# A fused decode block, forward and backward: hf, relu, mask and masked gradient made in three groups of column blocks

## The chip, the core and the metric

The kernel runs on one core of a Trainium2 chip. The metric is device microseconds (us) of one execution, as the median of several runs. The core has five engines that run their own instruction streams in order and wait for one another by semaphores: TensorE (PE, matmuls, with its weight loads shown apart as PEld), VectorE (DVE), ScalarE (ACT), GpSimd (POOL) and SyncE (SP, which here only issues transfers). Transfers run on 16 DMA engines that all queues share.

## The reference, cut to what matters

A pre-norm attention block over a key and value cache, a relu MLP, and the gradient of all inputs for a given output gradient. The batch B is 2, one query position, H = 32 heads of size 128, 4096 cached positions, model width D = 640 and MLP width Dff = 1728.

```python
h  = x + attention(layernorm(x), k_cache, v_cache, wq, wo)
h2 = h + relu(layernorm(h) @ w1) @ w2          # out_0
grads = vjp(x, k_cache, v_cache, wq, wo, w1, w2)(grad_out)   # out_1 .. out_7
```

Nearly all bytes are the cache (K and V, 1 MB for each of the 64 pairs of batch row and head) and its two gradients of the same size. The value cache is needed twice: for the output, and again for the gradient of the scores. The kernel keeps a few V tiles and loads 52 of them a second time.

## The kernel before, in words

**Two passes and a middle.** Pass 1 (`p1_iter`) has rows i = 0 to 65, one for each pair of batch row and head. A row transposes the K tile of pair i on PE, makes its scores, forms the products `pk` of the exponentials and K for pair i-1 on DVE (line 470, two halves), and multiplies V of pair i-2 on PE. Pass 2 (`p2_iter`, index j) reads V again (tile W), makes the score gradients and the two cache gradients gV and gK on DVE (line 844), and stores both through POOL's DMA queue. Between them, for each batch row b, lies the middle (`middle_gen(b)`): attention output, the layernorm, `hf` (the MLP's hidden row before the relu), relu, mask, the masked gradient `ghfc`, the gradient through w1, the layernorm's backward, and then for each group of heads the gradient through wo (`go_group`), without which pass 2 can't begin for those heads.

**Where a row stands.** The middle of batch row 0 runs beside rows 34 to 65 of pass 1; pass 2 begins at row `P2_AT` = 41 whatever the middle has done (what is missing for its first head is forced at that point) and then takes one step every second row. From there rows of pass 1 and steps of pass 2 alternate on all engines. After row 65 pass 2 runs alone, 14 of its 64 steps done; beside it run the middle of batch row 1, and then, once its sums over w1 are done (mark `("w1", 1)`), the generators `fin_gen` (outer products for the weight gradients, stores on ACT's queue) and `gx_gen` (gradient through wq).

**The order is written out by a small planner.** All engines get their instructions in the order in which the Python generators are stepped. A row of pass 1 has eight steps. After each, `bg_step` gives the middle a credit (0.8 a step from row 34 on, `RATES`); each `yield` of the middle costs what it says (0.25 for a column block of hf, 0.85 or 0.9 for a sum, 0.5 for a bare `yield`). `wait(n)` holds the middle for n steps (2n once `spread` is 2, from row 41 on). Sums over w1 and wo (`ttr`, line 678: multiply and add along a row) also need a slot (`turn()`): five a row in rows 34 to 40, two slots (with a pass-2 step) or one from row 41 on.

**The part around the change.** `hf` has 14 column blocks (13 full and one of 64). Each is five matmuls with one column (line 778). The relu (lines 781 and 783), mask (786) and masked gradient (787) follow on DVE over all 14. Then `wait(3)`. Then three times: `spread_some` turns five (the last time four) columns of `ghfc` into a row on all partitions, with PE transposes (line 645) and one ACT copy (line 647) into one half of `fbc`; and five sums over w1 (line 800). The layernorm's backward (`ln_bwd`) and `go_group` follow. In `go_group` each head is one sum over wo (line 699); then come a cast and a product (701, 703), two matmuls and four copies (`pair_rows`, 340 and 345), further matmuls (708, 712) and five small DVE operations (714 to 720).

**PSUM banks.** `pst` hands out banks by role. `hf_ps` and other small results use bank 7 (`mid`). The rows of `spread_some` use role `bc`: banks 2 and 7 by turns in rows 34 to 40, bank 7 alone for batch row 1.

**Buffers.** Loads of K, V and W take one of 13 large buffers (`ld`) and are issued by SP in one list as buffers come free (`pump`); K's buffer comes free after the second half of `pk`. Around row 41 some buffers go over to gV and gK (`g`), and later to `f` and `q`.

Of the kernel before, what the change touches and what calls it, by code (L numbers as in the profile page):

```python
# [9 lines left out]
ALU = mybir.AluOpType  # L10
# [5 lines left out]
def kernel(  # L16
# [20 lines left out]
    nc = tc.nc  # L37
# [6 lines left out]
    ND = D // 128  # L44
    NSC = Sk // 128
    NFF = Dff // 128
    F_rem = Dff - NFF * 128
    NF = NFF + (1 if F_rem else 0)
# [9 lines left out]
    def f_kc(c):  # L58
        return 128 if c < NFF else F_rem
# [11 lines left out]
    banks = {"tps": [0, 1], "sps": [2, 3, 4], "m": [5], "u": [6], "mid": [7], "bc": [7]}  # L71

    def pst(shape, dtype, role, name):

        k = banks[role].pop(0)
        banks[role].append(k)
        return ps.tile(shape, dtype, tag=f"bank{k}", bufs=1, name=name)
# [63 lines left out]
    def wait(n):  # L141

        end = step[0] + n * spread[0]
        while step[0] < end and not forced[0]:
            yield 0.0
        yield
# [34 lines left out]
    x2c = cols.tile([128, ND, B], BF16)  # L181
# [4 lines left out]
    acol = cols.tile([128, NF, B], BF16)  # L186
    ghfc = cols.tile([128, NF, B], BF16)
# [15 lines left out]
    ga = cols.tile([128, B, NF], FP32)  # L203
# [128 lines left out]
    w1_t = wts.tile([128, ND, Dff], BF16)  # L332
# [265 lines left out]
    def o_group():  # L598
        b, g = divmod(o_next[0], H // OG)
        hs = slice(g * OG, g * OG + OG)  # L600
        nc.vector.tensor_tensor(out=OU[:, b, hs], in0=OU[:, b, hs], in1=rt[:, b, hs], op=ALU.mult)
        nc.vector.tensor_copy(out=OFc[:, hs, b], in_=OU[:, b, hs])
        o_next[0] += 1

    def a_group():

        b, g = divmod(a_next[0], H // OG)
        a_ps = pst([128, ND], FP32, "mid", "a_ps")
        for c in range(ND):
            for h in range(g * OG, g * OG + OG):  # L610
                nc.tensor.matmul(a_ps[:, c:c + 1], lhsT=wo_t[:, h, c * 128:(c + 1) * 128], rhs=OFc[:, h, b:b + 1],
                                 start=(h == g * OG), stop=(h == g * OG + OG - 1))
        nc.vector.tensor_tensor(out=asum[:, b, :], in0=asum[:, b, :], in1=a_ps[:], op=ALU.add)
        a_next[0] += 1
# [10 lines left out]
    def u_out(b):  # L625

        t = pst([128, H], FP32, "mid", "uc_ps")
        nc.tensor.matmul(t[:], lhsT=u4[0], rhs=fold[:], start=True, stop=True)
        nc.vector.tensor_tensor(out=Uc[:, b, :], in0=t[:], in1=rt[:, b, :], op=ALU.mult)


    def wide_row(name):
        return cols.tile([128, B * D], BF16, tag="wide_row", name=name)

    def later_heads():

        return P_bf[:, B * H - D // NSC:, :].rearrange("p h s -> p (h s)")

    def spread_some(colsrc, c0, n, kc_of, dst):

        t = pst([128, D], BF16, "bc", "bcb_ps")
        w = 0
        for c in range(c0, c0 + n):
            kc = kc_of(c)
            nc.tensor.transpose(t[:, w:w + kc], colsrc[0:kc, c:c + 1].to_broadcast([kc, 128]), ident_bf[0:kc, 0:kc])
            w += kc
        nc.scalar.copy(out=dst[:, 0:w], in_=t[:, 0:w])
        return w
# [28 lines left out]
    def ttr(in0, in1, acc, width, junk, kc=128):  # L677
        nc.vector.tensor_tensor_reduce(out=junk[0:kc, 0:width], in0=in0, in1=in1, scale=1.0, scalar=0.0,  # L678
                                       op0=ALU.mult, op1=ALU.add, accum_out=acc)
# [3 lines left out]
    def turn():  # L683

        while slot[0] <= 0:
            yield 0.0
        slot[0] -= 1

    def one(src, b):
        return src[:, :, b]  # L690
# [61 lines left out]
    def middle_gen(b):  # L752
        if o_next[0] < (b + 1) * H // OG:
            o_group()
        u4[0] = wide_row("u")[:, 0:256].bitcast(FP32)
        nc.vector.tensor_reduce(out=u4[0], in_=u_bank[0][:].rearrange("p (s d) -> p d s", s=4),
                                axis=AX.X, op=ALU.add)
        yield
        while a_next[0] < (b + 1) * H // OG:
            if a_next[0] == o_next[0]:  # L760
                o_group()
                yield
                yield
            a_group()
            yield
        at_bf = small.tile([128, ND], BF16, tag="at_bf", bufs=1, name="at_bf")
        nc.vector.tensor_copy(out=at_bf[:], in_=asum[:, b, :])
        nc.vector.tensor_tensor(out=h1c[:, :, b], in0=xg32[:, b, :], in1=at_bf[:], op=ALU.add)
        h32 = small.tile([128, 1, ND], FP32, tag="h32", bufs=1, name="h32")
        nc.vector.tensor_copy(out=h32[:, 0, :], in_=h1c[:, :, b])  # L770
        yield ("a", b)
        u_out(b)
        yield from ln_fwd(h32[:], 1, x2c[:, :, b:b + 1], rstd2[:, b:b + 1])
        hf_ps = pst([128, NF], FP32, "mid", "hf_ps")
        for cf in range(NF):
            kc = f_kc(cf)
            for c in range(ND):
                nc.tensor.matmul(hf_ps[0:kc, cf:cf + 1], lhsT=w1_t[:, c, cf * 128:cf * 128 + kc],
                                 rhs=x2c[:, c, b:b + 1], start=(c == 0), stop=(c == ND - 1))
            yield 0.25  # L780
        nc.vector.tensor_scalar(out=acol[:, 0:NFF, b], in0=hf_ps[:, 0:NFF], scalar1=0.0, scalar2=None, op0=ALU.max)
        if F_rem:
            nc.vector.tensor_scalar(out=acol[0:F_rem, NFF, b:b + 1], in0=hf_ps[0:F_rem, NFF:NF],
                                    scalar1=0.0, scalar2=None, op0=ALU.max)
        mask = small.tile([128, NF], FP32, tag="mask", bufs=1, name="mask")
        nc.vector.tensor_single_scalar(out=mask[:], in_=acol[:, :, b], scalar=0.0, op=ALU.is_gt)
        nc.vector.tensor_tensor(out=ghfc[:, :, b], in0=ga[:, b, :], in1=mask[:], op=ALU.mult)
        yield from wait(3)
        fbc = wide_row("fbc")
        gx2 = small.tile([128, 1, ND], FP32, tag="gx2", bufs=1, name="gx2")  # L790
        gx2p = small.tile([128, ND, 3], FP32, tag="gx2p", bufs=1, name="gx2p")
        first_f = 0
        for k, n in enumerate((ND, ND, NF - 2 * ND)):
            row = fbc[:, (k % 2) * D:(k % 2 + 1) * D]
            w = spread_some(one(ghfc, b), k * ND, n, f_kc, row)
            yield
            for c in range(ND):
                yield from turn()
                part = w1_t[:, c, first_f:first_f + w]
                ttr(part, row[:, 0:w], gx2p[:, c, k:k + 1], w, part if b else later_heads())  # L800
                yield 0.85
            first_f += w
        nc.vector.reduce_sum(out=gx2[:, 0, :], in_=gx2p[:], axis=AX.X)
        yield ("w1", b)
        yield from ln_bwd(gx2[:], x2c[:, :, b:b + 1], rstd2[:, b:b + 1], gc[:, :, b:b + 1], gh1c[:, :, b:b + 1], 1)
        row = wide_row("hbc")
        hbc, junk = row[:, 0:D], row[:, D:2 * D]
        spread_some(one(gh1c, b), 0, ND, lambda c: 128, hbc)
        yield
        yield ("gh1", b)  # L810

        first = H - KEPT[b]
        bounds = [(first, first + 2), (first + 2, H)] if b == 0 else [(first, H)]
        bounds += [(h, min(first, h + GH)) for h in range(0, first, GH)]
        for h0, h1 in bounds:
            yield from go_group(b, h0, h1, hbc, junk)
        if b > 0:
            yield from mlp_out()
# [401 lines left out]
    for n, (i, j) in enumerate(plan):  # L1220
# [42 lines left out]
        if i is None:  # L1263
            spread[0] = 2
            at_k[0] = 1
            k = 0
# [28 lines left out]
        if i is not None and i in (H + 1, NP1 + 1):  # L1295
            bg.append((f"m{i // H - 1}", middle_gen(i // H - 1)))
# [41 lines left out]
```

## Time and profile before

| | |
|---|---|
| median of 3 runs | 889.0 us (888.36 to 891.58) |
| profiled execution, its own time | 888.48 us |
| span of the profiled execution | 886.3 us |
| busy share of the span: PE, DVE, ACT, POOL | 83%, 77%, 56%, 23% |
| bytes moved, mean rate | 361.85 MB, 408 GB/s |
| rows 34 to 41 of pass 1 begin at | 210.2, 217.4, 225.9, 232.0, 237.9, 243.6, 249.6, 256.0 us |

The row starts are read from the chain of waits, at each row's matmul of line 515. The span is what the trace shows from the first to the last instruction; the profiled execution's own time is 2.2 us longer. Tables by stretch give, for each stretch of the span, the busy time of each engine, the TensorE clock that was granted, the DMA engines' busy share and the rate. In lists in order of time the first two columns are start and duration in us. The brackets at the end say how long the engine was idle before the instruction, and what ended that.

### The profile page before, as it was taken

The numbers are of one execution on the slowest core, as the hardware profiler recorded it, in microseconds if no ns is written. First come the engines' busy times: TensorE is split into PE (matmuls) and PEld (weight loads), VectorE is DVE, ScalarE is ACT, GpSimd is POOL, SyncE is SP. The second block draws the span as 40 slices with busy tenths as digits, with TensorE's granted clock in tenths as the row PEclk, the third lists the DMA queues.
The fourth block names the chain that finished last, engine by engine and source line by source line (L and its number), as shares of the span: only waits on it lengthen the run. The fifth ranks groups of instructions, "written<-read, shape, count | busy, mean of one in ns | idle before, by whom it ended". The sixth has DMA issues, their size and how long they took to land.

```text
span 886.3 us, 24732 instructions
## 1 busy us (share of the span) xinstructions
PE 738.8 (83%) x10143; PEld 618.2 (70%) x10143; DVE 681.3 (77%) x1281; ACT 498.8 (56%) x1292; POOL 204.1 (23%) x358
## 2 busy tenths in 40 slices
PE   4999899999999997988868767787877899867690
PEld 4887788888887886877757656665656667564550
DVE  2666787877788896876778887878788689989861
ACT  1444343446776664654536767777656766545570
POOL 1344433343312010000011332222222111111220
PEclk9999999999999999998995655555566755555555
DMA  9999999999879999999999999999999999999996
GB/s 380 423 420 414 417 409 417 425 423 412 332 295 402 423 423 426 422 426 425 414 398 396 418 421 421 420 413 420 419 416 403 417 425 420 425 425 425 425 424 275
DMA packets 56289, 361.85 MB, mean 408 GB/s; under 512 B 5680, under 2 KB 11760, under 8 KB 15472
## 3 DMA queue, kind: packets, MB, share of 16 engines
q1 hardware_dynamic: 34520, 211.13, 57.8%
q0 software_dynamic: 18432, 134.23, 36.5%
q10 hardware_dynamic: 3224, 14.92, 4.1%
q8 instruction: 80, 1.31, 0.5%
q14 instruction: 33, 0.27, 0.1%
HBM read 211.11 MB, written 149.13 MB: 406 GB/s over the span
## 4 chain that ended last, share of the span: by engine, by line
PE 35%; DMA 34%; DVE 16%; ACT 7%; issue 5%; SPq 0%; POOL 0%; ACTq 0%; POOLq 0%; DVEq 0%
DMA Vt<-in_A_v_cache_dram 15%; PE t_ps L424 14%; DMA out_dram<-gK 11%; PE m_ps L460 9%; DVE gK L844 4%; DVE gV L844 4%; DMA out_dram<-gV 3%; ACT gV L930 3%; PE s_ps L437 3%; DMA wqs<-in_A_wq_dram 3%; DVE pk L470 2%; PE u_ps L498 2%; ACT t_sb L429 2%; PE dp_ps L437 2%; DVE gxj L678 2%
## 5 line engine op out<-in xcount | busy, mean ns | idle before, releaser
L429 ACT COPY t_sb<-t_ps 128x512 f32<-128x512 f32 x479 | 273.1, 587 | 192.4 <-PE t_ps L424 188.6
L437 PEld LDWEIGHTS <-t_sb 128*128 128x128 bf16 x4096 | 178.9, 102 | 63.8 <-ACT t_sb L429 36.2
L424 PE MATMUL t_ps<-ident_f,Wt 128*128 128x128 f32 x832 | 198.6, 389 | 0.9 <-ACT t_sb L429 0.9
L470 DVE TENSOR_TENSOR pk<-Kt,ep 128x2048 bf16<-128x2048 bf16 (+1 forms) x128 | 152.6, 1193 | 47.1 <-ACT ep L524 29.0
L460 PE MATMUL m_ps<-pk,Vt 128*128 128x129 bf16 x2048 | 172.0, 223 | 19.9 <-DMA Vt<-in_A_v_cache_dram 18.8
L844 DVE TENSOR_TENSOR gK<-rb,gsp 128x2048 bf16<-128x2048 bf16 x128 | 153.4, 1227 | 13.3 <-DMA out_dram<-gV 8.5
L460 PEld LDWEIGHTS <-Vt 128*128 128x128 bf16 x2048 | 125.6, 99 | 50.2 <-issue 28.4
L424 PEld LDWEIGHTS t_ps<-ident_f,Wt 128*128 128x128 f32 x832 | 138.2, 202 | 31.9 <-issue 25.2
L424 PE MATMUL t_ps<-ident_f,Kt 128*128 128x128 f32 x1024 | 156.0, 286 | 2.5 <-DMA Kt<-in_A_k_cache_dram 1.9
L844 DVE TENSOR_TENSOR gV<-rb,pp 128x2048 bf16<-128x2048 bf16 (+1 forms) x128 | 142.7, 1139 | 16.3 <-DMA out_dram<-gK 9.9
L486 POOL COPY pk<-ep 128x16 bf16<-128x16 bf16 x80 | 83.6, 1046 | 158.4 <-ACT ep L524 80.0
L424 PEld LDWEIGHTS t_ps<-ident_f,Kt 128*128 128x128 f32 x1024 | 113.9, 145 | 5.0 <-ACT t_sb L429 2.7
L437 PE MATMUL dp_ps<-gom,t_sb 128*128 128x2 bf16 x2048 | 96.0, 168 | 25.1 <-ACT t_sb L429 24.7
L931 POOL DMA_DIRECT2D out_dram<-gV x62 | 33.0, 533 | 305.3 <-DVE gsp L858 135.1
L437 PE MATMUL s_ps<-qm,t_sb 128*128 128x2 bf16 x2048 | 87.4, 164 | 1.5 <-DVE t_sb L427 1.5
L986 ACT CAST ot<-o_ps 128x512 bf16<-128x512 f32 (+3 forms) x152 | 67.5, 491 | 8.4 <-DMA out_dram<-ot 5.2
L588 ACT CAST MT<-m_ps 128x128 bf16<-128x128 f32 x64 | 17.0, 266 | 94.5 <-PE m_ps L460 94.4
L899 POOL DMA_DIRECT2D out_dram<-gK x53 | 28.2, 533 | 135.4 <-DVE gK L844 104.9
L882 ACT ACTIVATE rb<-dp_ps,rt 128x256 bf16<-128x256 f32 x64 | 30.2, 472 | 44.7 <-PE dp_ps L877 43.4
L678 DVE CUSTOM_DVE_ANT_0 hbc<-wo_t,hbc 128x640 bf16<-128x640 bf16 x64 | 52.8, 825 | 0.3
L678 DVE CUSTOM_DVE_ANT_0 gxj<-wqs,gqr 128x1024 bf16<-128x1024 bf16 x40 | 48.7, 1217 | 1.0 <-DMA wqs<-in_A_wq_dram 0.8
L930 ACT ACTIVATE gV<-rb,pa 128x128 bf16<-128x128 bf16 x152 | 46.5, 392 | 3.9 <-DMA out_dram<-gK 3.9
(205 smaller groups left out, 758.2 us busy)
## 6 DMA issues: line engine op xcount, KB each, us to landing
Kt<-in_A_k_cache_dram SPq DMA_DIRECT2D x64, 1024.0 KB, 19.4
Vt<-in_A_v_cache_dram SPq DMA_DIRECT2D x64, 1024.0 KB, 15.5
out_dram<-gV POOLq DMA_DIRECT2D x64, 1024.0 KB, 14.9
out_dram<-gK POOLq DMA_DIRECT2D x64, 1024.0 KB, 15.0
Wt<-in_A_v_cache_dram SPq DMA_DIRECT2D x52, 1024.0 KB, 11.6
wq_t<-in_A_wq_dram SPq DMA_DIRECT2D x5, 1024.0 KB, 7.8
wo_t<-in_A_wo_dram SPq DMA_DIRECT2D x4, 1280.0 KB, 17.6
wqs<-in_A_wq_dram SPq DMA_DIRECT2D x5, 1024.0 KB, 22.3
```

The source lines that it names most:

```text
L424: nc.tensor.transpose(t_ps[:, j, :], natf[:, 2 * cc:2 * cc + 2, :].rearrange("p c k -> p (c k)"), ident_f[:])
L429: nc.scalar.copy(out=t_sb[:], in_=t_ps[:])
L437: nc.tensor.matmul(dst[:, sc:sc + 2], lhsT=v[:, j, :, par], rhs=vecs[:, par, :], start=(par == 0), stop=(par == 1))
L460: nc.tensor.matmul(r["m"][:, 0:129], lhsT=r["V"][:, sc, :], rhs=r["pk"][sc // HALF][:, sc % HALF, 0:129], start=(sc == 0), stop=(sc == NSC ...
L470: nc.vector.tensor_tensor(out=p["pk"][k][:, 0:n, 0:128].rearrange("p s (a two) -> p s a two", two=2), in0=p["K"][:, sl, :].rearrange("p s ...
L486: nc.gpsimd.tensor_copy(out=col, in_=e)
L678: nc.vector.tensor_tensor_reduce(out=junk[0:kc, 0:width], in0=in0, in1=in1, scale=1.0, scalar=0.0, op0=ALU.mult, op1=ALU.add, accum_out=acc)
L844: nc.vector.tensor_tensor(out=pairs_view(dst[:, sl, :]), in0=row.rearrange("p (a two) -> p a two", two=2)[:, None, :, :].to_broadcast([128 ...
L882: nc.scalar.activation(out=rb[:], in_=bank[:, 128:384], func=ACT.Copy, scale=rt[:, b, h:h + 1])
L930: nc.scalar.activation(out=gV[:, NSC - act + k, :], in_=c["rb"][:, 0:128], func=ACT.Copy, scale=pa[:, k:k + 1])
L931: nc.gpsimd.dma_start(out=natural(out_3, b, h), in_=gV[:])
L986: nc.scalar.copy(out=ot[0:P, k, n0:n0 + nn], in_=o_ps[0:P, 0:nn])
```

## The change

The 14 column blocks are cut in three groups (5, 5 and 4), the same that the sums use. The generator now gives: hf of group 0, its relu, mask and masked gradient; hf of group 1, the spread of group 0, relu, mask and masked gradient of group 1; hf of group 2 and its relu part; then the sums of group 0, and spread and sums of groups 1 and 2. `wait(3)` is gone, and the bare `yield` between the first spread and its sums. The roles of the PSUM banks are set so that the spread of group 0 doesn't use the bank of `hf_ps`: for batch row 0 the list is turned until bank 7 is not first, for batch row 1 `bc` is bank 5 until the sums are done. `P2_AT` stays 41. The number of matmuls, copies, sums and transfers stays the same; DVE has 12 more small operations (six for each batch row).

```diff
-        for cf in range(NF):
-            kc = f_kc(cf)
-            for c in range(ND):
-                nc.tensor.matmul(hf_ps[0:kc, cf:cf + 1], lhsT=w1_t[:, c, cf * 128:cf * 128 + kc],
-                                 rhs=x2c[:, c, b:b + 1], start=(c == 0), stop=(c == ND - 1))
-            yield 0.25
-        nc.vector.tensor_scalar(out=acol[:, 0:NFF, b], in0=hf_ps[:, 0:NFF], scalar1=0.0, scalar2=None, op0=ALU.max)
...
-        yield from wait(3)
...
-        for k, n in enumerate((ND, ND, NF - 2 * ND)):
+        parts = [(0, ND), (ND, 2 * ND), (2 * ND, NF)]
+
+        def hf_part(k):
+            for cf in range(*parts[k]):
+                kc = f_kc(cf)
+                for c in range(ND):
+                    nc.tensor.matmul(hf_ps[0:kc, cf:cf + 1], lhsT=w1_t[:, c, cf * 128:cf * 128 + kc],
+                                     rhs=x2c[:, c, b:b + 1], start=(c == 0), stop=(c == ND - 1))
+                yield 0.25
+
+        def relu_part(k):
+            c0, c1 = parts[k]
+            full = min(c1, NFF)
+            nc.vector.tensor_scalar(out=acol[:, c0:full, b], in0=hf_ps[:, c0:full], scalar1=0.0, scalar2=None, op0=ALU.max)
...
+            nc.vector.tensor_single_scalar(out=mask[:, c0:c1], in_=acol[:, c0:c1, b], scalar=0.0, op=ALU.is_gt)
+            nc.vector.tensor_tensor(out=ghfc[:, c0:c1, b], in0=ga[:, b, c0:c1], in1=mask[:, c0:c1], op=ALU.mult)
+
+        def spread_part(k):
+            c0, c1 = parts[k]
             row = fbc[:, (k % 2) * D:(k % 2 + 1) * D]
-            w = spread_some(one(ghfc, b), k * ND, n, f_kc, row)
-            yield
+            return row, spread_some(one(ghfc, b), c0, c1 - c0, f_kc, row)
+
+        def sum_part(k, row, w):
+            first_f = parts[k][0] * 128
             for c in range(ND):
                 yield from turn()
                 part = w1_t[:, c, first_f:first_f + w]
                 ttr(part, row[:, 0:w], gx2p[:, c, k:k + 1], w, part if b else later_heads())
                 yield 0.85
-            first_f += w
+
+        if b == 0:
+            while banks["bc"][0] == 7:
+                banks["bc"].append(banks["bc"].pop(0))
+        else:
+            banks["bc"] = [5]
+        yield from hf_part(0)
+        relu_part(0)
+        yield from hf_part(1)
+        first = spread_part(0)
+        relu_part(1)
+        yield from hf_part(2)
+        relu_part(2)
+        yield from sum_part(0, *first)
+        for k in (1, 2):
+            row, w = spread_part(k)
+            yield
+            yield from sum_part(k, row, w)
+        if b > 0:
+            banks["bc"] = [7]
```

## The prediction

> **What bounds the kernel now.** I read the page first, then a table by stretch, then the chain of waits, then DVE in order of time where the chain leaves the transfers.
>
> From the page, the DMA share and the rate in 40 slices of 22.2 us:
>
> ```profile
> DMA  9999999999879999999999999999999999999996
> GB/s 380 423 420 414 417 409 417 425 423 412 332 295 402 423 423 426 422 426 425 414 398 396 418 421 421 420 413 420 419 416 403 417 425 420 425 425 425 425 424 275
> ```
>
> Transfers run at some 420 GB/s nearly throughout. The hole is at slices 10 and 11 (222 to 266 us). The stretches, with busy times of PE, PEld, DVE, ACT and POOL, then clock, DMA share and GB/s:
>
> ```profile
> 204.00:222.00 18.00, 18.00 (x339) 16.30 (x339) 13.76 (x43) 12.20 (x36) 6.80 (x11) 1.00 0.99 409
> 222.00:230.00 8.00, 7.77 (x129) 7.00 (x126) 3.23 (x10) 4.18 (x12) 1.25 (x3) 0.79 0.94 359
> 230.00:263.00 33.00, 32.04 (x526) 27.93 (x526) 30.59 (x83) 26.15 (x77) 8.42 (x20) 1.00 0.78 300
> 280.00:440.00 160.00, 143.37 (x2359) 127.28 (x2362) 125.22 (x258) 90.48 (x249) 13.90 (x30) 0.95 1.01 423
> 440.00:500.00 60.00, 45.57 (x646) 40.37 (x644) 47.05 (x93) 33.84 (x91) 11.93 (x26) 0.72 0.99 399
> 655.00:680.00 25.00, 21.05 (x204) 17.92 (x203) 22.77 (x46) 15.14 (x35) 6.24 (x11) 0.50 0.99 401
> 680.00:865.00 185.00, 153.95 (x1381) 111.14 (x1380) 154.69 (x206) 117.90 (x252) 31.10 (x65) 0.57 1.01 423
> ```
>
> In 230 to 263 us (rows 37 to 41) PE is busy 97% and DVE 93%, and the transfers wait for compute. From 280 us on the transfers bound the time again. Since the bytes are fixed, a microsecond lost before 263 us is lost at the end. The chain shows the hand-over (start, duration in us):
>
> ```profile
> 259.40 1.14 DVE pk L470
> 260.53 1.14 DVE gV L844
> 261.76 1.13 DVE pk L470
> 262.92 7.59 DMA Vt<-in_A_v_cache_dram
> ```
>
> Row 41's second `pk` product frees the buffer, and a V load issued at 262.92 starts the bound stretch. What DVE does up to that product decides.
>
> **The change part by part.** The built programs show what moves. In rows 36 to 41 DVE gets 22 sums before that last `pk` in place of 19: group 0's first two stand in row 36 ahead of its first `pk`, everything behind comes 3 to 4 planner steps sooner, and in the rows before 41, with their five slots, the three head sums of heads 29 to 31 now fit, which stood in rows 41 and 42. Their tail (lines 701 to 720) comes from rows 42 and 43 to rows 40 and 41. DVE in order of time, before:
>
> ```profile
> 226.11 0.29 DVE L517 TENSOR_REDUCE nb<-s_ps 128x1 f32<-128x128 f32 x1 [1.35 <-PE s_ps L515]
> 227.04 0.83 DVE L470 TENSOR_TENSOR pk<-Kt,ep 128x1280 bf16<-128x1280 bf16 x1 [0.64 <-ACT ep L524]
> 228.63 0.83 DVE L678 CUSTOM_DVE_ANT_0 P_bf<-w_t,fbc 128x640 bf16<-128x640 bf16 x1 [0.77 <-ACT fbc L647]
> ...
> 258.57 0.82 DVE L678 CUSTOM_DVE_ANT_0 hbc<-wo_t,hbc 128x640 bf16<-128x640 bf16 x1
> ...
> 262.91 0.81 DVE L678 CUSTOM_DVE_ANT_0 hbc<-wo_t,hbc 128x640 bf16<-128x640 bf16 x1
> ...
> 269.98 0.81 DVE L678 CUSTOM_DVE_ANT_0 hbc<-wo_t,hbc 128x640 bf16<-128x640 bf16 x1
> ```
>
> The sums at 258.57, 262.91 and 269.98 are the three that come forward; others take the two slots of row 41.
>
> *Added before the hand-over.* Three sums at a pitch of 0.86 (250.13 to 250.99): 2.6 us. The tail of heads 28 to 31: 0.28 (270.84 to 271.12), copies 0.50 (273.05), five small operations 0.74 (278.23 to 278.97): 1.5. Together 4.1 us of DVE.
>
> *What of it is covered.* DVE waits 4.6 us in rows 36 to 41 (1.35, 0.64, 0.77, 0.54, 0.32, 0.41, 0.57). The first two sums (1.7 us) find only the 0.64 and 0.77 of row 36, because `fbc` is ready sooner. The other waits are for hand-overs with PE or ACT, and the moved steps bring such hand-overs themselves. I lay the rows out by hand with the durations of before, and give how much later each row's `nb` (line 517) stands:
>
> - Row 37, +0.6: 1.7 us of sums less 1.4 us of waits, and 0.3 us by which row 35 ends later on PE (the five transposes now stand there).
> - Row 38, +0.65: the same work in row 37.
> - Row 39, +2.1: five sums of 448 columns in place of two of 640 and three of 448 (-0.4 us), but `ln_bwd`'s eight operations (0.51 and 0.96 us) now end row 38; PE, done with row 39's transposes, waits about 1 us for them.
> - Row 40, +3.0: row 39 loses `ln_bwd` and two 448 sums (2.8 us); it gains two head sums (1.7), cast, product and copies (0.8), some 0.8 of waiting for `hbc`, whose spread stands between row 39's matmuls, and a short wait of PE at `pr_ps`.
> - Row 41, +4.8: four head sums in place of three (0.86), `d_ps` awaited at the row's start (0.5), and `pr_ps` at its end ahead of the transposes that `nb` needs.
> - Last `pk` of row 41, +5.5: the five small operations (0.74).
>
> So the term is +5.5 us. Its bounds: 0 if all 4.6 us of waits could be filled, and +8 if the small waits (0.5 to 1 each) come in all six rows as the longest seen here (1.35). I take 5.5, since the sums alone fill what is free.
>
> *Row 35.* Three relu, mask and gradient groups in place of one: six more small operations at 0.18 (line 787), 1.1 us, in a row where DVE waits 1.64, 0.56 and 1.35 us. The first group stands ahead of the second `pk`, which ends 1.5 us later, and so does the release of its K buffer. Nobody is behind it: the chain has no transfer between 224 and 262 us. Between 0 and +1.5; I take 0. ACT's first copy of `fbc` (0.70) now stands ahead of the copies that free `m_ps` (lines 588, 589); PE's transposes of the next row cover it: 0, at most +0.7. The dropped `wait(3)` removes no instruction; what it gave was the place of all that follows.
>
> *Given back.* The middle of batch row 0 ends in row 60, not 63. The small operations of heads 24 and 25 (444.66 to 445.38, 0.7 us) lie on the chain at 440 to 445 us: -0.7. The sums gone from rows 60 to 63 lie beside transfers at 423 GB/s: 0.
>
> *Batch row 1.* Its sums start seven planner steps sooner, so `fin_gen` and `gx_gen` begin one step of pass 2 (about 7 us) sooner. Stores on ACT's queue go out earlier, and on SP's queue one w2 load falls behind two wq loads, a row store behind W and wq loads; POOL's order is unchanged. Bytes are the same and the rate is 419 to 423 GB/s around, so 0. The last POOL stores follow pass 2, not `fin_gen`: 0 at the end. The pause of W loads before the hand-out of buffers is three planner steps shorter; 655 to 680 us lacks (423 - 401) / 423 x 25 = 1.3 us, of which I take -0.5. Six more small operations, 1.1 us, stand beside transfers: 0, and +1.1 if that cover is gone.
>
> *Sum:* 5.5 - 0.7 - 0.5 = +4.3. The profiled execution took 888.5 us in its own time, 0.5 below the median of 889.0. Against the median: **893.3 us**.
>
> *The clock.* In 222 to 230 us the granted clock is 0.79: after the hf matmuls it is 0.50 for 3 us, though PE is nowhere idle for over 0.25 us, and eight transposes take 1.97 us in place of 1.07. The waits of about 1 us that I put into rows 38 to 41 lie among work at 1.00, and before's waits there (0.3 us) had no drop. The Trainium skill (TensorE: Matmul & The Clock Gate, section "Part 1: The HAM clock gate") puts the drop to half clock at an idle window of about 3.4 us. By that rule waits of 1 us cost nothing more and the sum stays 893.3; the row at 222 us doesn't fit it, and by that row a drop may come without such a gap, as in the second rival.
>
> **The rivals.**
> *1. DVE's free time takes most of it.* For: 4.6 us of waits against 4.1 of work. Against: only 1.4 us lies where the new sums stand. With two thirds filled the lag is 1.5 and the time 889.0 + 1.5 - 1.2 = 889.3.
> *2. The lag grows by PE's clock.* If the waits in rows 38 to 41 bring two drops like the one at 224 us, each costs 0.9 (transposes) and 0.4 (m_ps, 1.02 for 0.63): +2.6, and 895.9. Against: clock 1.00 throughout 230 to 263 us.
> *3. The other side: faster.* The middle ends three rows before pass 1, `fin_gen` starts sooner, and so the hole where pass 2 goes on alone (440 to 500 us, 399 for 423 GB/s, 3.4 us) and the one at 655 to 680 (1.3) close: -4.7. It decides where row 41 lags under 4.7 us; with no lag at all it gives 884.3. For: both holes are compute waits. Against: at 455 to 480 us the waits are for stores, which nothing here changes, and the lag.
>
> That the change doesn't do what it says is excluded by the order of the built program.
>
> **How the numbers follow.** Forecast 0.50, rival 1 0.22, rival 2 0.13, rival 3 0.15. A measurement tells about 0.5% (4.4 us) from no change: 893.4 is the upper edge, 884.6 the lower. The forecast's own range is 891 to 897; it lies on the edge, and I count 0.38 of it as slower, as the hand layout leaves out small waits, and 0.12 as same. Rival 1 is all same; rival 2 slower; rival 3 0.12 faster, 0.03 same. So faster 0.12, same 0.37, slower 0.51. The range reaches from 887 (rival 1 with a bit of rival 3) to 898 (8 us, and the two unlikely row-35 terms in part).
>
> **What would show it.** In the changed kernel's profile: in row 36 two sums ahead of the first `pk`, row starts later by 2 us at row 39 and 4 to 5 at row 41, the V load that starts the bound stretch near 268.4 us, the rate of 230 to 263 us below 300 GB/s, and from 290 us on the same rate, so that the lag stays to the end. The forecast is wrong if row 41 lags by under 2 us, if rows 42 to 65 make the lag up (then the transfers weren't the bound there), or if 440 to 500 us rises to 420 GB/s.

## The result, and the profile after

The changed kernel takes 895.55 us (median of 11 runs, 893.76 to 899.9), the kernel before 890.92 us on the same chip (11 runs, 887.28 to 894.36). The ratio is 1.0075 with a 95% interval of 1.0057 to 1.0092, so it is slower by 6.7 us (5.1 to 8.2, from ratio times 889). The ratio is the measurement's own estimate from these runs; the two medians alone give 1.0052, which is 4.6 us. The document goes by the ratio throughout. The profiled execution took 896.82 us in its own time, with a span of 894.6.

The page of the changed kernel, DMA share and rate in 40 slices, now of 22.4 us:

```profile
DMA  9999999999869999999999999999999999999995
GB/s 379 425 419 415 416 405 417 426 423 396 323 236 369 414 423 423 426 425 424 425 386 408 420 420 421 416 422 417 421 415 390 424 424 423 426 426 425 423 425 238
```

The hole stands in the same slices and is deeper (236 where before had 295, and 369 in the slice behind it). The rest differs little. The table by stretch of the changed kernel (PE, PEld, DVE, ACT, POOL, then clock, DMA share, GB/s):

```profile
222.00:230.00 8.00, 7.68 (x165) 6.84 (x164) 5.57 (x19) 5.15 (x16) 1.27 (x4) 1.00 0.92 359
230.00:263.00 33.00, 27.36 (x444) 23.94 (x441) 28.42 (x85) 22.94 (x70) 6.79 (x19) 0.98 0.82 313
263.00:280.00 17.00, 16.70 (x266) 14.91 (x265) 13.90 (x27) 12.28 (x37) 2.96 (x4) 0.93 0.58 220
280.00:440.00 160.00, 145.82 (x2414) 128.10 (x2412) 127.73 (x264) 91.65 (x252) 14.45 (x29) 0.96 1.01 422
440.00:500.00 60.00, 44.74 (x637) 40.26 (x638) 43.38 (x88) 30.11 (x79) 10.85 (x24) 0.69 1.00 403
655.00:680.00 25.00, 21.29 (x212) 17.96 (x211) 23.25 (x45) 14.09 (x30) 7.69 (x11) 0.50 0.97 400
680.00:865.00 185.00, 145.84 (x1348) 105.12 (x1346) 153.17 (x206) 112.87 (x243) 30.39 (x64) 0.59 1.01 423
```

Two things are to be seen. From 280 us on, the rates are those of before within 1%, so what was lost ahead stays lost. And in 230 to 263 us PE is busy 27.4 us where it had 32.0, DVE 28.4 where it had 30.6: more work had been put on DVE, and both engines wait more. Over 230 to 280 us the transfers move (33 x 313 + 17 x 220) = 14.1 MB, before (33 x 300 + 17 x 391) = 16.5 MB; the missing 2.5 MB are 5.9 us at 423 GB/s.

The chain of waits at the hand-over in the changed kernel (start, duration):

```profile
266.43 1.14 DVE pk L470
267.57 1.14 DVE gV L872
268.70 0.09 DVE P_bf L564
268.79 1.13 DVE pk L470
269.92 0.03 DVE rmax L576
269.95 7.65 DMA Vt<-in_A_v_cache_dram
```

It is the same chain as before: the second `pk` of row 41 frees the buffer, and the V load that opens the bound stretch starts at 269.95, not 262.92. Of these 7.0 us, 1.9 were there already at row 35, where both kernels have the same order of instructions (`nb` of row 35 at 219.40, before 217.50); so I take that part as scatter between executions. All times at the hand-over are given below as counted from row 35's `nb`: 45.42 us before, 50.55 us in the changed kernel.

DVE of the changed kernel in order of time, at the start of row 36 and at the start of row 41 (brackets: idle time before the instruction, and what ended it):

```profile
227.48 0.29 DVE L517 TENSOR_REDUCE nb<-s_ps 128x1 f32<-128x128 f32 x1 [0.45 <-PE s_ps L515]
227.69 0.81 DVE L678 CUSTOM_DVE_ANT_0 P_bf<-w_t,fbc 128x640 bf16<-128x640 bf16 x1
...
228.55 0.87 DVE L678 CUSTOM_DVE_ANT_0 P_bf<-w_t,fbc 128x640 bf16<-128x640 bf16 x1
...
229.34 0.82 DVE L470 TENSOR_TENSOR pk<-Kt,ep 128x1280 bf16<-128x1280 bf16 x1
...
259.46 1.19 DVE L470 TENSOR_TENSOR pk<-Kt,ep 128x2048 bf16<-128x2048 bf16 x1
260.57 0.16 DVE L701 CAST goc<-go 128x4 bf16<-128x4 f32 x1
...
262.07 0.29 DVE L517 TENSOR_REDUCE nb<-s_ps 128x1 f32<-128x128 f32 x1 [0.53 <-PE s_ps L515]
263.73 1.23 DVE L872 TENSOR_TENSOR gV<-rb,pp 128x2048 bf16<-128x2048 bf16 x1 [1.36 <-ACT rb L910]
```

The two sums of group 0 stand ahead of row 36's first `pk`, as the order of the built program had said. In row 40 the cast `goc` of four heads is queued behind the long `pk`, and PE, which has its `pr_ps` matmuls next in its own order, waits for it. PE of the changed kernel:

```profile
252.69 0.20 PE L340 MATMUL pr_ps<-goc,sel 128*128 128x2 bf16 x2 [1.84 <-DVE goc L701]
...
260.79 0.20 PE L340 MATMUL pr_ps<-goc,sel 128*128 128x4 bf16 x2 [2.21 <-DVE goc L701]
260.89 1.06 PE L424 MATMUL t_ps<-ident_f,Kt 128*128 128x128 f32 x8
261.79 0.24 PE L515 MATMUL s_ps<-neg_ident,rmax 128*128 128x128 bf16 x1
261.85 1.05 PE L460 MATMUL m_ps<-pk,Vt 128*128 128x129 bf16 x8
```

Eight `m_ps` matmuls took 1.05 us here against 0.63 at full clock. The granted clock by microsecond says why:

```profile
261.00:262.00 1.00, 1.00 (x11) 0.99 (x11) 0.53 (x5) 0.39 (x1) 0.00 (x0) 0.93 1.02 426
262.00:263.00 1.00, 1.00 (x12) 1.00 (x10) 0.29 (x1) 0.68 (x2) 0.00 (x0) 0.50 0.38 156
263.00:264.00 1.00, 1.00 (x8) 1.00 (x7) 0.27 (x1) 0.47 (x1) 0.00 (x0) 0.50 0.00 0
264.00:265.00 1.00, 1.00 (x9) 0.98 (x10) 1.00 (x2) 0.91 (x4) 0.00 (x0) 0.50 0.00 0
265.00:266.00 1.00, 1.00 (x25) 0.96 (x23) 0.90 (x6) 0.84 (x2) 0.00 (x0) 0.86 0.00 0
```

A microsecond after PE resumes, its clock is at half for 3.4 us. DVE's `gV` waits 1.36 us for `rb` there, before 0.57. The same places before, PE at the end of row 39 and in row 41 and then DVE in row 41:

```profile
252.08 0.19 PE L340 MATMUL pr_ps<-goc,sel 128*128 128x2 bf16 x2
256.07 0.63 PE L460 MATMUL m_ps<-pk,Vt 128*128 128x129 bf16 x8
```

```profile
256.57 0.29 DVE L517 TENSOR_REDUCE nb<-s_ps 128x1 f32<-128x128 f32 x1
257.43 1.23 DVE L844 TENSOR_TENSOR gV<-rb,pp 128x2048 bf16<-128x2048 bf16 x1 [0.57 <-ACT rb L882]
```

### The profile page after: what moved, and what is told of

Same layout as the page of the kernel before. It is cut to its first block, busy times and chain, and to the rows that moved or that the text cites. A ratio compares the mean times of both kernels' runs of the same rounds, so it can differ in the third digit from the quotient of the medians.

```text
span 894.6 us, 24744 instructions
## 1 busy us (share of the span) xinstructions
PE 744.2 (83%) x10143; PEld 621.1 (69%) x10143; DVE 683.7 (76%) x1293; ACT 497.6 (56%) x1292; POOL 199.7 (22%) x358
## 4 chain that ended last, share of the span: by engine, by line
PE 39%; DMA 27%; DVE 17%; ACT 9%; issue 6%; ACTq 0%; POOL 0%; SPq 0%; POOLq 0%; DVEq 0%
PE t_ps L424 16%; DMA Vt<-in_A_v_cache_dram 13%; PE m_ps L460 9%; DMA out_dram<-gV 7%; DMA out_dram<-gK 4%; DVE gK L872 4%; DVE gV L872 4%; ACT gV L958 3%; PE s_ps L437 3%; ACT t_sb L429 3%; DMA wqs<-in_A_wq_dram 3%; DVE pk L470 2%; PE u_ps L498 2%; DVE gxj L678 2%; PE dp_ps L437 2%
## 5 line engine op out<-in xcount | busy, mean ns | idle before, releaser
L424 PE MATMUL t_ps<-ident_f,Kt 128*128 128x128 f32 x1024 | 158.0, 288 | 2.9 <-DMA Kt<-in_A_k_cache_dram 2.2
L872 DVE TENSOR_TENSOR gV<-rb,pp 128x2048 bf16<-128x2048 bf16 (+1 forms) x128 | 142.6, 1140 | 14.1 <-DMA out_dram<-gK 9.1
L486 POOL COPY pk<-ep 128x16 bf16<-128x16 bf16 x80 | 81.8, 1024 | 165.8 <-ACT ep L524 88.4
```

Of the source, the lines that this page charges most:

```text
L424: nc.tensor.transpose(t_ps[:, j, :], natf[:, 2 * cc:2 * cc + 2, :].rearrange("p c k -> p (c k)"), ident_f[:])
L486: nc.gpsimd.tensor_copy(out=col, in_=e)
L872: nc.vector.tensor_tensor(out=pairs_view(dst[:, sl, :]), in0=row.rearrange("p (a two) -> p a two", two=2)[:, None, :, :].to_broadcast([128 ...
```

## The experiments

The theory was that the loss is made in rows 36 to 41, by the DVE work that the planner now puts ahead of the hand-over. The rivals: the split itself (twelve more small operations, another order of PE in row 35), the change in batch row 1, and later on: that any added DVE work would cost as much, wherever it stands. All experiments were timed against the kernel before on the same chip; where a ratio is turned into us it is times 889.

**The wait put back (e1).** The changed kernel, with the three-step wait and the bare `yield` again for batch row 0, behind the third relu part.

```diff
         relu_part(2)
+        if b == 0:
+            yield from wait(3)
+            yield
         yield from sum_part(0, *first)
```

> The changed kernel with the hold of three planner steps put back for batch row 0, between the last relu group and the first sums: hf, relu, mask and masked gradient stay in three groups, but every sum from row 36 on stands in the row in which it stood before (3, 5, 5, 2 and 3 sums in rows 36 to 40). Theory 1 (what costs is the place of the sums and their tails in rows 36 to 41): back to before, ratio 0.998 to 1.001. Rival A (the split itself costs: six more small operations, the later release of a K buffer in row 35, the spread's place): stays near 1.0075. Rival B (batch row 1's earlier start costs): stays near 1.0075, since batch row 1 is as in the changed kernel.

Measured: 889.78 us, ratio 1.0013 (0.9996 to 1.0031), V load 44.26 us behind row 35's `nb`. The three groups stay, DVE's sums in rows 36 to 41 are again those of before, and nearly all of the loss is gone. The split itself costs 1.2 us with zero within the interval.

**Only the wait dropped (e2).** The kernel before, without three groups.

```diff
-        yield from wait(3)
+        if b > 0:
+            yield from wait(3)
```

> The kernel before, with nothing changed but that batch row 0 no longer holds for three planner steps ahead of its sums; no groups, batch row 1 as before. DVE then has the sums of rows 36 to 41 in the rows of the changed kernel (5, 5, 5, 2 and 4 in rows 36 to 40). Theory 1: as slow as the changed kernel, 1.006 to 1.009 (a little more than the changed one if PE waits for the relu in row 35). Rival A: 1.000 to 1.002. Rival B: 1.000 to 1.002.

Measured: 896.92 us, ratio 1.0095 (1.0069 to 1.0121), V load at 53.90. The order of the sums alone, without groups, gives a loss as large as the change's. In this execution PE waited 1.84 and 1.77 us for `goc`, and its clock fell to 0.50 after both.

**Heads 28 to 31 held (e3).** The changed kernel; the group of four heads waits for row 41, rows 36 to 39 stay as changed.

```diff
         for h0, h1 in bounds:
+            while b == 0 and h0 == first + 2 and step[0] < 8 * P2_AT and not forced[0]:
+                yield 0.0
             yield from go_group(b, h0, h1, hbc, junk)
```

> The changed kernel, but the group of heads 28 to 31 of batch row 0 may not begin before row 41. The four head sums and the tail of row 40 go behind; rows 36 to 39 stay as in the changed kernel. Before row 41's last pk stand 18 sums (before: 19, changed: 22) and one tail (changed: two). Theory 1: most of the lag goes, about 1 us stays at most, ratio 0.998 to 1.002. If the sums ahead of pk in row 36, or the layernorm's backward at the end of row 38, were the costly part: 1.003 to 1.006. Rivals A and B: 1.0075.

Measured: 892.44 us, ratio 1.0042 (1.0022 to 1.0061), V load at 46.83. So of the 50.55 - 44.26 = 6.3 us between the changed kernel and e1, 3.7 go with the four sums of heads 28 to 31 and their tail in rows 40 and 41, and 2.6 stay with what moved in rows 36 to 39. The ratio misses the range of theory 1 and lies in the other one, 1.003 to 1.006. The 2.6 us that stay aren't added work: from row 35's `nb` to the V load DVE is busy 37.97 us in e3 and 38.34 in e1, but idle 8.86 and 5.92. PE waits 1.84 us for `goc` in row 39, and DVE, with no sums left to do in row 40, then waits for PE:

```profile
255.83 0.18 DVE L563 RECIPROCAL rt<-s_ps 128x4 f32<-128x4 f32 x1 [1.52 <-PE s_ps L558]
```

So the amount of DVE work ahead of the hand-over isn't the whole cause; the hand-overs with PE that moved along with it cost time of their own.

**The second pass one row sooner (e4).** The changed kernel with pass 2 beginning at row 40.

```diff
-    M0_ITERS = 7
+    M0_ITERS = 6
```

> The changed kernel with the second pass begun at row 40 in place of 41 (six rows of the middle ahead of it, not seven). Heads 28 to 31 then fall behind the start. Theory 1: one row of 6.4 us at 360 GB/s less in the compute-bound stretch (worth 1.0 us of transfers) and a lag of 2 to 3 us at its end in place of 5: ratio to the kernel before 0.999 to 1.004, below the changed kernel by 0.004 to 0.008. If the lag didn't come from compute in these rows, it stays at 1.0075.

Measured: 892.09 us, ratio 1.0034 (1.0017 to 1.0051). It wins back half, and isn't better than before. Its V load isn't comparable with the others, since the hand-over is another one.

**Batch rows apart (e5, e6).** The three groups for one batch row, the old middle for the other.

```diff
+        if b == 1:      # e5; in e6: if b == 0
...
+        else:
...
```

> The three groups for batch row 1 only; the middle of batch row 0 as before. Theory (the whole difference is made ahead of the hand-over at row 41): V load within 0.5 us of before, counted from row 35, and ratio 0.998 to 1.002. Rival (batch row 1's change has a price or a gain of its own): outside that, with the difference in the stretches behind 650 us.

> The three groups for batch row 0 only; the middle of batch row 1 as before. Theory (what counts is the DVE work that the planner puts ahead of the hand-over at row 41): rows 36 to 41 have the same sums as in the changed kernel, so the V load that starts the bound stretch stands about 5 us later than before, counted from row 35, and the ratio is that of the changed kernel, 1.005 to 1.009. Rival (batch row 1's change, its bank and its six more small operations, costs part): under 1.004, the rest to be found in batch row 1.

Measured: e5 887.75 us, ratio 0.9995 (0.9975 to 1.0014), V load at 43.71; e6 897.92 us, ratio 1.0097 (1.0072 to 1.0122), V load at 52.13. Batch row 0 makes all of the loss; batch row 1 makes no difference that is measured. e5's V load is 1.7 us earlier than before's, more than the expected 0.5; the table below shows that this arises ahead of row 37. e6 lies over its expected range: its clock fell in row 41 too, and stayed at half for 6.8 us, not 3.4, so that behind `gV` the last `pk` of row 41 had to wait as well, for `m_ps`:

```profile
265.33 1.23 DVE L903 TENSOR_TENSOR gV<-rb,pp 128x2048 bf16<-128x2048 bf16 x1 [1.02 <-ACT rb L941]
...
271.25 1.23 DVE L470 TENSOR_TENSOR pk<-Kt,ep 128x2048 bf16<-128x2048 bf16 x1 [0.84 <-PE m_ps L460]
```

**Less ahead of the hand-over than before (e7).** e1 with the hold of e3: one head sum fewer ahead of row 41's `nb` than in the kernel before.

> The changed kernel with the three-step wait put back for batch row 0 and, besides, the sums of heads 28 to 31 held until row 41 (one head sum fewer ahead of row 41 than before, three fewer than the changed kernel in row 40, and their tail behind). Theory: less DVE work ahead of the hand-over than before, so the V load stands 2 to 3 us earlier than before from row 35 on, and the ratio is 0.996 to 0.999, under the 1.001 of the kernel with the wait alone. Rival (the total of moved work doesn't matter, or what is held comes back later on the path): 1.001 or more.

Measured: 889.64 us, ratio 1.0005 (0.9985 to 1.0024), V load at 44.29, the same as e1 (44.26). The expectation was wrong: taking a sum of 0.8 us away there brings nothing. DVE of e7 at that place:

```profile
256.78 0.29 DVE L517 TENSOR_REDUCE nb<-s_ps 128x1 f32<-128x128 f32 x1 [0.33 <-PE s_ps L515]
257.96 1.23 DVE L877 TENSOR_TENSOR gV<-rb,pp 128x2048 bf16<-128x2048 bf16 x1 [0.90 <-ACT rb L915]
```

Ahead of this `nb` the kernel before had a sum and no wait; now there is a wait for PE of 0.33, and the wait for `rb` grew from 0.57 to 0.90. Before, PE was busy 97% in 230 to 263 us and DVE 93%, so I take PE to be as much a bound there as DVE. So the two directions aren't alike: less DVE work gains nothing, more of it costs.

**Useless work on DVE, early and late (e8, e9).** The kernel before, with a reduction over 128x640 elements in each of four rows; its result isn't used.

```diff
             bg_step(1, 0.0)
+            if i in (37, 38, 39, 40) and k == 4:      # e9: rows 50 to 53
+                nc.vector.tensor_reduce(out=negdot[:, H - 1, B - 1:B], in_=wo_t[:, 0, 0:D], axis=AX.X, op=ALU.max)
```

> The kernel before, with one useless reduction over 128x640 elements on DVE added in each of rows 37 to 40 (result unused), four times about 0.7 to 0.9 us = 2.8 to 3.6 us. Nothing else moves. Theory: DVE work ahead of the hand-over counts nearly one to one: V load 2 to 3.5 us later from row 35 on, ratio 1.002 to 1.004. Rival (DVE's free time takes it; the loss of the change is in the moved order itself or in the transfers): V load under 1 us later, ratio 1.000 to 1.001.

> The same four reductions in rows 50 to 53, where transfers run at 423 GB/s and DVE is busy 78% of the time. Theory: covered by transfers, ratio 0.999 to 1.001, V load as before. Rival (DVE work costs the same anywhere): 1.002 to 1.004.

The line of the reduction in e8 (x4, ns least, median, most):

```profile
L1296 DVE TENSOR_REDUCE negdot<-wo_t x4: 809/814/820, 236.2 to 255.3; 128x1 f32<-128x640 bf16 x4
```

Measured: e8 890.44 us, ratio 1.0024 (1.0007 to 1.0042), V load at 47.84, so 2.4 us later for 4 x 0.814 = 3.3 us of work; counted from row 37's `nb`, ahead of the first reduction, it is 2.65 us, some 0.7 in each of rows 37 to 39 and 0.5 in row 40. e9 890.81 us, ratio 1.002 (1.000 to 1.004), V load at 45.84. The V loads tell the two apart, the times don't: e9's ratio lies above its theory's range and at the edge of the rival's, so at four reductions the times of this pair are inconclusive.

**Three times the dose (e10, e11).** Twelve reductions in the same four early rows, and twelve in rows 44 to 55.

```diff
+            if i in (37, 38, 39, 40) and k in (2, 4, 6):                     # e10
+            if i is not None and 44 <= i < 56 and k == 4:                    # e11
```

> The kernel before with twelve useless reductions over 128x640 on DVE (0.81 us each as measured, 9.7 us; result unused), three in each of rows 37 to 40. Theory: four of them moved the V load by 2.4 us, the free time of DVE being used up by the first ones; twelve move it by 8 to 9.5 us, and the ratio is 1.008 to 1.011. Rival (DVE's work is mostly absorbed): under 1.005.

> The same twelve reductions, one in each of rows 44 to 55, beside transfers at 423 GB/s. Theory: covered, V load within 0.5 us of before from row 35 on, ratio 0.999 to 1.003. Rival (the 1.002 of the four late ones was a real price and grows with their number): 1.006 or more.

Measured: e10 894.72 us, ratio 1.0075 (1.0048 to 1.0103), V load at 50.89; e11 888.41 us, ratio 1.0008 (0.9986 to 1.0029), V load at 46.98. With 12 x 0.814 = 9.8 us of work the place decides: ahead of the hand-over it costs 6.7 us, behind it nothing that can be measured. So the 1.002 of e9 was no price. e10's time is a little under its expected range, and so is its V load, 7.2 us later than e5's where 8 to 9.5 were expected. Not all of that is DVE work as such: PE waited 1.75, 2.07 and 1.14 us for DVE's `rmax`, and behind the second wait its clock was at half for 3.4 us. e11's V load is 1.6 us later though its first reduction stands at 285 us, behind that load; the last section says where those 1.6 come from.

**The casts ahead of `pk` (e12).** The changed kernel with one swap on DVE in rows 39 and 40; all engines have the same instructions.

```diff
             ttr(wo_t[:, h0 + k, :], hbc, go32[:, k:k + 1], D, junk)
-            yield 0.9
+            if not (early and k == n - 1):
+                yield 0.9
...
         nc.vector.tensor_tensor(out=pr[:, 0:n], in0=goc[:, hs, b], in1=OU[:, b, hs], op=ALU.mult)
+        if early:      # early = b == 0 and h0 >= H - KEPT[0]
+            yield 0.9
```

> The changed kernel with one swap on DVE in rows 39 and 40: the cast `goc` and the product `pr` (lines 701 and 703) stand ahead of the second `pk` product in place of behind it. The same instructions on all engines. In the changed kernel PE, in its own order, waited 1.84 and 2.21 us for these casts, ran at half clock for 3 us behind the second wait, and DVE then waited 0.50, 0.40, 0.53 and 1.36 us for PE and ACT. Theory A (that round trip, DVE to PE and back, is a part of the loss of its own beside the added DVE work): PE's waits fall to about 0.7 and 1.1 us, no half clock in row 41, the V load 2 to 3 us earlier than in the changed kernel from row 35 on (48 to 48.7 us behind row 35's nb at clock 1.00 in 222 to 230 us, where the changed kernel has 50.6), ratio 1.003 to 1.006. Theory B (DVE is full, and PE's waits only mirror it): V load within 0.8 us of the changed kernel's, ratio 1.006 to 1.009.

Measured: 893.9 us, ratio 1.0062 (1.0039 to 1.0084), V load at 48.97. PE of e12, and then DVE in row 41:

```profile
250.09 0.20 PE L340 MATMUL pr_ps<-goc,sel 128*128 128x2 bf16 x2 [0.82 <-DVE goc L703]
...
257.61 0.20 PE L340 MATMUL pr_ps<-goc,sel 128*128 128x4 bf16 x2 [1.13 <-DVE goc L703]
```

```profile
259.50 0.29 DVE L517 TENSOR_REDUCE nb<-s_ps 128x1 f32<-128x128 f32 x1
260.56 1.23 DVE L876 TENSOR_TENSOR gV<-rb,pp 128x2048 bf16<-128x2048 bf16 x1 [0.76 <-issue]
```

PE's waits fell from 1.84 and 2.21 to 0.82 and 1.13, the clock stayed at 1.00 in rows 39 to 41, and the V load came 1.6 us sooner than in the changed kernel: 1.0 at row 41's `nb` and 0.6 behind it. That lies between the two theories: the round trip from DVE to PE and back is a part of the loss; the swap takes away 1.6 of 6.8 us, though it halves PE's waits and doesn't end them. The times of e12 and of the changed kernel aren't told apart by their intervals.

**All together.** Behind the hf matmuls the clock was at half for 0, 3.4 or 6.8 us, by execution, and the V load moves with it. So each kernel is set beside one with the same length there whose order of instructions up to the hand-over is that of before: e5, before itself or e11. The column behind it counts from row 37's `nb`.

| kernel | half clock behind hf (us) | V load behind row 35 (us) | later by | behind row 37 (us) | time (us, 95%) |
|---|---|---|---|---|---|
| e5, batch row 1 only | 0 | 43.71 | reference | 30.61 | -0.4 (-2.2 to 1.2) |
| before | 3.4 | 45.42 | reference | 30.61 | 0 |
| e11, twelve late | 6.8 | 46.98 | reference | 30.62 | 0.7 (-1.2 to 2.6) |
| e1, wait put back | 0 | 44.26 | 0.6 | 30.63 | 1.2 (-0.4 to 2.8) |
| e7, e1 and heads held | 0 | 44.29 | 0.6 | 30.64 | 0.4 (-1.3 to 2.1) |
| e9, four late | 3.4 | 45.84 | 0.4 | 30.61 | 1.8 (0.0 to 3.6) |
| e8, four early | 3.4 | 47.84 | 2.4 | 33.26 | 2.1 (0.6 to 3.7) |
| e3, heads 28 to 31 held | 0 | 46.83 | 3.1 | 32.48 | 3.7 (2.0 to 5.4) |
| e12, casts first | 0 | 48.97 | 5.3 | 34.62 | 5.5 (3.5 to 7.5) |
| e6, batch row 0 only | 3.4 | 52.13 | 6.7 | 36.78 | 8.6 (6.4 to 10.8) |
| changed kernel | 0 | 50.55 | 6.8 | 36.20 | 6.7 (5.1 to 8.2) |
| e2, wait dropped alone | 6.8 | 53.90 | 6.9 | 36.93 | 8.4 (6.1 to 10.8) |
| e10, twelve early | 0 | 50.89 | 7.2 | 37.85 | 6.7 (4.3 to 9.2) |

With the order of before, rows 37 to 41 take 30.61 or 30.62 us in four executions, so the scatter lies ahead of row 37. The lag of one load at the hand-over gives the time of the whole kernel one to one within the intervals, which are 3 to 5 us wide, over edits as different as a moved order and useless work. The single executions say it more sharply: from the V load to the end of the span each of them has 623.1 to 626.4 us left (e4 apart, with its other hand-over), though the load itself starts anywhere from 261.2 to 273.8 us. No version beat the kernel before.

From row 35's `nb` to the V load, DVE of the changed kernel is busy 42.43 us where e5 has 37.62, and idle 8.12 us where e5 has 6.09. So of the 6.8 us 4.8 are work and 2.0 are waits. In e12 the work is the same and 0.5 of waits is left; in e3 nearly all is waits (2.8 of 3.1).

## Why the prediction was right, and where its terms were off

The forecast was slower by 4.3 us, 893.3 us within 887 to 898, and that is how it went: 895.55 us, by the ratio 6.7 us slower. The main mechanism held: e1 and e2 show that the order in rows 36 to 41 makes the loss, e8 to e11 that most of a microsecond of DVE ahead of the hand-over counts and one behind it doesn't. The 4.1 us of DVE work that the forecast added up are there, too (42.43 us in the changed kernel, 38.34 in e1, which has the split but the old places of the sums). Three smaller terms were off and are answered below. That the two medians lie 4.6 us apart, so close to 4.3, I take for luck: the ratio says 6.7, and the V load beside e5's 6.8.

*The rows.* `nb` of each row, later than in another kernel, counted from row 35. The changed kernel had no half clock behind the hf matmuls and before had 3.4 us of it, so beside before it has a head start; e5 had none, and e6 3.4 us like before.

| row | forecast | changed kernel beside before | changed kernel beside e5 | e6 beside before |
|---|---|---|---|---|
| 37 | +0.6 | -0.5 | +1.3 | +0.5 |
| 38 | +0.65 | -0.4 | +1.3 | +0.6 |
| 39 | +2.1 | +1.3 | +3.0 | +2.3 |
| 40 | +3.0 | +2.1 | +3.8 | +3.1 |
| 41 | +4.8 | +3.6 | +5.3 | +4.6 |
| V load | +5.5 | +5.1 | +6.8 | +6.7 |

The steps from row to row came out as laid out by hand: +1.7 into row 39 (forecast 1.45), +0.8 into row 40 (0.9), +1.5 into row 41 (1.8). Single waits were met as well: PE waited 1.14 us for `ln_bwd` (forecast about 1), DVE 0.86 for `hbc` (0.8) and 0.40 for `d_ps` (0.5).

*The term that was mis-sized* is the last one, from row 41's `nb` to the last `pk`: 0.7 forecast (five small operations), 1.5 measured in the changed kernel and 2.1 in e6. The five operations took the 0.7; the other 0.8 is `gV`'s longer wait for `rb`. The waits of PE at `pr_ps`, of which the forecast called the first short and gave the second no size, were 1.84 and 2.21 us, and behind the second the clock fell to half. With the casts ahead, shorter waits and no drop (e12), 0.6 of the 0.8 go. That is the second rival, which the sum had left out: it had two drops at 1.3 each, there was one, for 0.8 at most. In e2 both came. The prediction held against this rival that the clock was 1.00 throughout in 230 to 263 us; that was a reading of a stretch without such waits.

*Row 35*, costed at 0 with +1.5 as its bound: e1 keeps the split and has its V load 0.6 us later than e5, all but 0.02 of it by row 37; e7 has the same. So the price at the hand-over is small but not nothing, though the times of e1 and e7 don't show it clear of zero.

*Given back*, 0.7 and 0.5: nothing of it is seen. The changed kernel is 6.8 us late at the hand-over and 6.7 at the end; in 655 to 680 us the rate is 400 GB/s where it was 401. e5's -0.4 would fit the 0.5, but its interval holds zero. Such small terms can't be shown or refuted by these runs. With the longer last term (0.8) and the split (0.6) put in and these two (1.2) left out, the sum of 4.3 becomes 6.9.

*The first rival*, that DVE's free time takes most of it, falls: counted from row 37, of e8's 3.3 us of work 0.6 was absorbed, of e10's 9.8 us 2.5. *The third rival*, faster, falls: 440 to 500 us went from 399 to 403 GB/s, and to 403 in the same stretch moved by the lag (447 to 507 us), not to 420. The middle of batch row 0 did end sooner (its last small operation on DVE at 421.0 us, before at 445.3); the rate there hardly rose with it.

*One sign named was wrong*: the rate in 230 to 263 us didn't fall under 300 GB/s, it was 313. The lag shifts the empty part of the hole out of that window, into 263 to 270 us; in 230 to 280 us it fell from 331 to 281. A window with edges taken from one kernel cuts the other's stage in another place.

## What to carry to other kernels

Where a stretch bound by compute hands over to one bound by transfers, the lag of the first load behind the hand-over is the price of an edit (in this kernel within the intervals of all runs), and work that a planner moves ahead of that point costs, though it is free a few microseconds later. Dropping a wait from a generator frees no time by itself: what it changes is which sums fall ahead of the hand-over, so read the new order first, count the waits between engines that move along with the work, and look for a small cast that another engine awaits and that is queued behind a long product. Before work is taken from the fullest engine, look whether the next one is just as full: here the sum that e7 took away turned into waits for PE and ACT. And when single executions are compared, count from a point behind their scatter: here from row 37, where four executions with the same order agree within 0.01 us.

## What the runs showed of the hardware that was not expected

The granted clock behind the burst of hf matmuls is a matter of the single execution. e5 and e11 have the same order of instructions there as before; their tables for 222 to 230 us, first e5, then e11:

```profile
222.00:230.00 8.00, 8.00 (x155) 7.35 (x153) 5.05 (x15) 5.54 (x18) 1.78 (x4) 1.00 0.93 371
```

```profile
222.00:230.00 8.00, 7.49 (x105) 7.27 (x103) 1.91 (x8) 3.25 (x9) 1.20 (x4) 0.58 0.97 372
```

One ran at 1.00, one at 0.58, before at 0.79; row 37's `nb` stands at -1.7, +1.6 and 0 us beside one another. So the 1.6 us of e11's V load, and a part of the scatter that single profiles show, come from there. PE need not be idle for that: in e8, whose clock was 0.79 there, it was busy 8.00 of 8 us.

Where the clock fell, it stayed at half for 3.4 us or twice that: 3.4 in before and in row 41 of the changed kernel, 6.8 in row 41 of e6 and in e11 (counted from the share of full speed in steps of 0.1 us). Waits of PE of 1.84 to 1.89 us were followed by half clock in e2 and not in the changed kernel, e3, e4 or e6; the two of 2.21 us (changed kernel, e6) both were. The Trainium skill (TensorE: Matmul & The Clock Gate, section "Part 1: The HAM clock gate") tells of a free-running window of about 3.4 us. The lengths of 3.4 and 6.8 us agree with one and two such windows.

The traces show that it is a matter of phase whether a given wait is caught. In e2 half clock begins at 225.50, 256.22 and 266.46 us, in e6 at 226.73 and 264.27; the distances are 9.0, 3.0 and 11.0 times 3.41 us. With such windows laid back from the start of a drop in the same execution, five waits of PE in rows 37 to 41 lay with 1.77 us or more in one window, and the clock fell at that window's end (2.21 in the changed kernel, 1.90 of 2.21 in e6, 1.84 and 1.77 in e2, 2.07 in e10). Four were cut by a window's edge, with 1.42 us or less on either side, and it didn't fall (1.84 in the changed kernel and in e6, 1.89 in e4, 1.75 in e10). What lies between 1.42 and 1.77 us no run shows. e3 had no drop to count from.

The same section of the Trainium skill lets the clock fall after at least one idle window, and that doesn't agree: no wait ahead of these drops was longer than 2.21 us. Why the clock falls behind the hf matmuls without any gap stays open; no run here tried it. Whether the split makes that fall rarer isn't shown either: with the old order in row 35 two of seven executions had none (e5, e10), with the groups in batch row 0 five of seven (all but e4 and e6), and these are single executions.
